# Sixteen weight conversions: one of four VectorE operations goes to GpSimd

## The chip, the cores and the metric

The kernel runs on one core of one Trainium2 chip. The metric is the device time of one execution in microseconds (us). The core has a matrix engine (TensorE, PE in the profile, with its weight loads as PEld), VectorE (DVE), ScalarE (ACT), GpSimd (POOL) and SyncE (SP), which issues the DMAs. Each engine works through its own list of instructions in order, and waits at the head of the list until the data and the buffer of the next instruction are free. SBUF is the on-chip working memory. PSUM is the memory into which TensorE writes; GpSimd has no operand there in this kernel.

## The reference

Attention over 32 memory slots, for 8 batches of 8 heads, 576 positions and 64 dimensions, and then two feed-forward layers on 4608 tokens:

```
a   = softmax over the positions of phi            # [b, h, 576, 32]
k_m, v_m = a^T k, a^T v                            # [b, h, 32, 64]
p   = softmax over the 32 slots of q k_m^T / 8
x   = p v_m                                        # 4608 x 512
h = x @ w1;  x = (h - tanh(h)) @ w2                # 512 -> 2048 -> 512
h = x @ w3;  out = where(h > 0, h, exp(min(h, 0)) - 1) @ w4
```

The weights arrive as 64-bit floats. The kernel builds 32-bit floats from their two 32-bit words.

## The kernel before, in words

**Weights.** `convert` (line 41) makes a 128x512 tile of 32-bit floats of a tile `raw` of 64-bit words. The high word is clamped and shifted to give the sign, the exponent and the upper bits of the mantissa, and the low word gives the rest. ScalarE takes the absolute value of the high word into a PSUM tile `cv_m` (line 48), VectorE clamps it (line 50), shifts and masks it (line 51), puts the sign in (line 54) and the low bits (line 57). In a "whole" conversion (the first eight tiles of `w1`) that is the weight. In the others the result stands in an SBUF tile `cv_a`, ScalarE rounds it to the high half of the weight (line 62), and GpSimd subtracts that to get the low half (line 64). `cv_m` has one buffer, `cv_a` two, `raw` three. There are 64 conversions; the first 16 are those of `w1` and `w2` for the first half of the hidden columns (four pairs of tiles of each).

**Attention.** 16 units, each one batch and four heads (line 118), with the tiles named in the profile: `cmax`, `mT`, `dmax`, `bmax` for the maximum over positions, `a`, `km`, `kk`, `vbd` for the memories, `pq`, `qT`, `sc`, `s`, `smax`, `pT`, `phl` for the scores and their softmax. A unit ends with the DMA of `phl` to `p` (units 0 and 1, line 246) and to DRAM, from where later blocks load `p` (line 329).

**Layer 1.** 64 blocks of 288 tokens with a quarter of the hidden columns each. A block has two halves. In each: `h_ps` on TensorE (line 375), `t`, `u`, `s`, `big` on ScalarE (lines 386 to 397), `v` on GpSimd (393), three operations on VectorE (402 to 404), `g` on ScalarE and GpSimd (410, 411), and `x_ps` on TensorE (423), which runs four products behind. `vw` (line 360) is the product of memories and `w1`, which `h_ps` needs. **Layer 2** follows from block 60 on.

**The order of the work.** The program is written out in one thread. Units and conversions are Python generators: each `yield` ends a stage, and `Staged.round()` takes every live generator one stage on. The loop over blocks calls `cv.round()` and `cv.half()` for conversions and `units.round()` twice in every half. Unit starts stand in a table of round numbers (`units.at`). Where a block needs weights that are not converted yet, `need` calls `cv.round()` until they are, and in block 1 each such call takes the units on by a round too. So the number of stages of a conversion decides how its instructions and those of the units stand among those of the blocks.

Of the kernel before, what the change touches and what calls it, by code (L numbers as in the profile page):

```python
# [8 lines left out]
F32 = mybir.dt.float32  # L9
F32R = mybir.dt.float32r  # L10
I32 = mybir.dt.int32
U32 = mybir.dt.uint32
ACTF = mybir.ActivationFunctionType
ALU = mybir.AluOpType
# [21 lines left out]
def r32(ap):  # L36
    return ap.bitcast(F32)


def convert(nc, pool, psum, raw, dst, whole=False):  # L40

    words = raw.bitcast(U32)
    w_lo, w_hi = words[:, 0::2], words[:, 1::2]
    lo_lim = 2.0 ** -15
    hi_lim = float.fromhex("0x1.fffffep+16")
    m = psum.tile(list(w_hi.shape), F32, tag="c", name="cv_m")
    mu = m.bitcast(U32)
    nc.scalar.activation(m, w_hi.bitcast(F32), ACTF.Abs)
    yield
    nc.vector.tensor_scalar(m, m, hi_lim, lo_lim, op0=ALU.min, op1=ALU.max)  # L50
    nc.vector.tensor_scalar(mu, mu, 3, 0x3FFFFFFF, op0=ALU.logical_shift_left, op1=ALU.bitwise_and)
    yield
    a = pool.tile(list(w_hi.shape), F32, tag="a", name="cv_a")
    nc.vector.scalar_tensor_tensor(mu, w_hi, 0xC0000000, mu, op0=ALU.bitwise_and, op1=ALU.bitwise_or)
    if whole:
        a = dst()
    nc.vector.scalar_tensor_tensor(a.bitcast(U32), w_lo, 29, mu, op0=ALU.logical_shift_right, op1=ALU.bitwise_or)
    if whole:
        return
    yield  # L60
    hi, lo = dst()
    nc.scalar.activation(hi, a, ACTF.Copy)
    yield
    nc.gpsimd.tensor_tensor(lo, a, r32(hi), op=ALU.subtract)  # L64
# [484 lines left out]
def moe_kernel(tc, q, k, v, phi, w1, w2, w3, w4, out):  # L549
    nc = tc.nc  # L550
    with ExitStack() as top, tc.manual_schedule():
# [15 lines left out]
        cv_p = new(l1b, "cv", 2, side="right")  # L567
# [3 lines left out]
        cv_ps = new(top, "ps_c", 1, space=PSUM)  # L571
# [20 lines left out]
        def conv(layer, kind, pg, c, lead=2):  # L592

            w = {("i", 1): w1, ("o", 1): w2, ("i", 2): w3, ("o", 2): w4}[kind, layer]
            raw = raw_p.tile([128, 512], mybir.dt.int64, tag="raw", name="raw")
            if kind == "i":
                src = w.rearrange("(k p) f -> p k f", p=128)[:, 2 * c:2 * c + 2, 256 * pg:256 * pg + 256]
                nc.sync.dma_start(out=raw.rearrange("p (a f) -> p a f", a=2), in_=src)
            else:
                r0 = 256 * pg + 128 * c  # L600
                nc.sync.dma_start(out=raw, in_=w[r0:r0 + 128, :])
            for k in range(lead + 1):
                yield k == lead
            staged, whole = [], (layer, kind) == (1, "i") and pg < 4

            def dst():
                if layer == 1:
                    ws = wi if kind == "i" else wo
                    if c == 0:
                        pg2, odd = divmod(pg, 2)  # L610
                        if kind == "i":
                            ws[pg] = [wt_p[pg2 % 2].tile([128, 4, 256], F32 if whole else F32R, tag=f"wi{odd}a", name="w1")]
                            if not whole:
                                ws[pg].append(wt_p[2].tile([128, 4, 256], F32R, tag=f"wl{pg}", name="w1"))
                        else:
                            pool, tags = (wt_p[odd], "wi0b wi1b") if pg2 == 2 else (wt_p[pg2], f"wo{odd}a wo{odd}b")
                            ws[pg] = [pool.tile([128, 2, 512], F32R, tag=t, name="w1") for t in tags.split()]
                    if whole:
                        return part(ws[pg][0], c)
                    return [part(t, c) for t in ws[pg]]  # L620
                staged.append(wst_p[0].tile([128, 2, 512], F32R, tag="wst", name="wst"))
                return staged[-1][:, 0], staged[-1][:, 1]

            yield from convert(nc, cv_p, cv_ps, raw, dst, whole)
            converted.add((layer, kind, pg, c))
            if layer == 2:
                yield
                nc.sync.dma_start(out=w_dram[kind][pg, :, :, 512 * c:512 * c + 512], in_=r32(staged[-1]))

        conv_pair = lambda layer, kind, pg: [conv(layer, kind, pg, c) for c in range(2)]  # L630
        conv_l1 = lambda kind, *pgs: [g for pg in pgs for g in conv_pair(1, kind, pg)]
        conv_l2 = [g for pg in range(NPG) for kind in "io" for g in conv_pair(2, kind, pg)]
# [8 lines left out]
        for what in "phi", "kv", "q0", "q1":  # L641
            at0.load(0, what)
            at1.load(1, what)
        cv_first = [conv(1, "i", k // 2, k % 2, 0) for k in range(3)]
        cv = Staged([conv(1, "i", 1, 1)] + conv_l1("o", 0, 1), 2)
        cv.wait = 5
        for k, g in enumerate(cv_first):
# [140 lines left out]
        for bi, (ss, bp, sub, j) in enumerate(blocks):  # L788
# [50 lines left out]
            for i in range(2):  # L839
                pg = 2 * sw + i  # L840
# [107 lines left out]
```

## Time and profile before

| | before |
|---|---|
| median of three runs | 1695.24 us (1695.19 to 1697.84) |
| profiled execution, its own time | 1694.74 us |
| its span, first to last instruction | 1693.0 us |
| TensorE busy | 1616.4 us, 95% |
| VectorE, ScalarE, GpSimd busy | 1190.3, 930.6, 760.0 us |
| mean granted TensorE clock | 0.988 of full speed |

Busy shares are means over stages that differ: in the first 165 us the attention, the conversions and the first blocks share all engines, and TensorE is busy least there. A row of idle time names what ended it.

### The profile page before, as it was taken

The page shows a single profiled execution, that of the slowest core. Times are in us where ns is not written, and L with a number is a line of the kernel's source. Part 1 is how long each engine was busy: PE and PEld are TensorE (multiplying, and loading weights), DVE is VectorE, ACT ScalarE, POOL GpSimd, SP SyncE. Part 2 cuts the span into 40 slices and gives each one's busy share as a digit, 9 for nine tenths or more (in the row PEclk, how much of TensorE's full clock was granted, in tenths as well). Part 3 has the DMA queues.
Part 4 walks back from the last instruction along what each step waited for, and adds up shares of the span by engine and source line. Part 5 has one row for each costly group of instructions (what it writes and reads, how often), then busy time and mean ns, then how long its engine had stood idle before and what let it go on. Part 6 is the DMA issues. An engine that isn't in the chain of part 4 may idle for free.

```text
span 1693.0 us, 26754 instructions
## 1 busy us (share of the span) xinstructions
PE 1616.4 (95%) x9986; PEld 1400.3 (83%) x9986; DVE 1190.3 (70%) x1730; ACT 930.6 (55%) x1677; POOL 760.0 (45%) x540
## 2 busy tenths in 40 slices
PE   6778999899998999999999999999999999999998
PEld 4556888787898999999999888888888888888886
DVE  4887778677989999999865655655555556555554
ACT  2466777677788898988853333333333333333332
POOL 1245666566666776767652322222323223223222
PEclk9889999999999999999999999999999999999999
DMA  8875667576565566665588321212121212121100
GB/s 204 216 201 167 202 192 220 175 212 211 192 207 168 170 215 220 218 219 205 188 274 309 100 74 38 75 50 63 50 73 40 75 40 72 51 75 50 31 7 25
DMA packets 140922, 236.10 MB, mean 139 GB/s; under 512 B 8184, under 2 KB 102392, under 8 KB 138744
## 3 DMA queue, kind: packets, MB, share of 16 engines
q1 hardware_dynamic: 140792, 234.39, 43.6%
q8 instruction: 79, 1.29, 0.3%
q14 instruction: 51, 0.42, 0.1%
HBM read 158.73 MB, written 74.45 MB: 138 GB/s over the span
## 4 chain that ended last, share of the span: by engine, by line
PE 75%; DVE 8%; ACT 5%; DMA 4%; issue 4%; POOL 3%; SPq 0%; ACTq 0%; POOLq 0%; DVEq 0%
PE h_ps L484 24%; PE o_ps L526 23%; PE x_ps L423 16%; PE h_ps L375 8%; DMA raw<-in_moe_w_in_dram 2%; DVE s L403 1%; PE vw_ps L344 1%; PE vw_ps L360 1%; DMA phi<-in_phi_dram 1%; ACT t L386 1%; DVE h_ps L402 1%; DMA kv<-in_v_dram 1%; POOL v L393 1%; PE km L170 1%; DVE s L404 1%
## 5 line engine op out<-in xcount | busy, mean ns | idle before, releaser
L423 PE MATMUL x_ps<-g,w 128*128 128x288 f32 x3072 | 441.6, 297 | 12.9 <-POOL w L64 4.7
L510 POOL TENSOR_TENSOR e<-hm,e 128x512 fp32r<-128x512 f32 x144 | 187.0, 1299 | 577.0 <-ACT e L509 533.7
L423 PEld LDWEIGHTS x_ps<-g,w 128*128 128x128 f32 x3072 | 417.1, 189 | 26.9 <-ACT x L430 7.5
L484 PE MATMUL h_ps<-x,wi 128*128 128x512 f32 (+1 forms) x1920 | 424.6, 371 | 0.0
L526 PE MATMUL o_ps<-wo,e 128*128 128x512 f32 x1728 | 422.8, 393 | 0.7 <-POOL e L510 0.7
L484 PEld LDWEIGHTS h_ps<-x,wi 128*128 128x128 f32 x1920 | 336.1, 188 | 68.0
L526 PEld LDWEIGHTS o_ps<-wo,e 128*128 128x128 f32 x1728 | 323.3, 188 | 75.4 <-POOL e L510 1.1
L495 ACT ACTIVATE t_ps<-hm 128x512 f32<-128x512 f32 x144 | 86.7, 602 | 504.8 <-DVE hm L494 504.8
L393 POOL TENSOR_TENSOR v<-t,u 128x576 f32<-128x576 f32 x128 | 183.1, 1430 | 155.7 <-ACT u L387 141.3
L501 DVE SCALAR_TENSOR_TENSOR hm<-hm,t_ps 128x512 f32<-128x512 f32 x144 | 99.0, 688 | 201.2 <-ACT hm L496 201.2
L375 PE MATMUL h_ps<-p,vw 128*128 128x288 f32 x1536 | 234.9, 303 | 5.0 <-DVE s L404 3.0
L411 POOL TENSOR_TENSOR g<-s,g 128x576 fp32r<-128x576 f32 x128 | 201.2, 1572 | 82.9 <-ACT g L410 74.3
L375 PEld LDWEIGHTS h_ps<-p,vw 128*128 128x128 f32 x1536 | 214.3, 192 | 16.1 <-issue 10.4
L494 DVE TENSOR_SCALAR hm<-h_ps 128x512 f32<-128x512 f32 x144 | 99.6, 692 | 129.3 <-PE h_ps L484 128.6
L403 DVE SCALAR_TENSOR_TENSOR s<-s,v 128x576 f32<-128x576 f32 x128 | 141.8, 1108 | 7.3 <-POOL v L393 7.2
L386 ACT ACTIVATE t<-h_ps 128x576 f32<-128x576 f32 x128 | 83.3, 651 | 84.0 <-PE h_ps L375 36.6
L404 DVE COPY_PREDICATED s<-big,h_ps 128x576 f32<-128x576 uint32 x128 | 106.5, 832 | 12.1 <-DVE s L403 0.5
L388 ACT ACTIVATE s<-u,bias 128x576 f32<-128x576 f32 x128 | 99.6, 778 | 25.4 <-POOL g L411 15.8
L503 DVE TENSOR_TENSOR hm<-hm,h_ps 128x512 f32<-128x512 f32 x144 | 98.9, 687 | 5.0
L502 DVE SCALAR_TENSOR_TENSOR hm<-hm,t_ps 128x512 f32<-128x512 f32 x144 | 98.9, 687 | 5.0
L402 DVE TENSOR_TENSOR h_ps<-h_ps,t 128x576 f32<-128x576 f32 x128 | 96.7, 755 | 3.2 <-ACT u L387 3.2
L496 ACT ACTIVATE hm<-hm 128x512 f32<-128x512 f32 x144 | 91.1, 632 | 14.0 <-ACT t_ps L495 1.1
(96 smaller groups left out, 1703.7 us busy)
## 6 DMA issues: line engine op xcount, KB each, us to landing
x_dram<-x SPq DMA_DIRECT2D x128, 288.0 KB
xr<-x_dram SPq DMA_DIRECT2D x72, 512.0 KB
p<-p_dram SPq DMA_DIRECT2D x62, 576.0 KB
raw<-in_moe_w_in_dram SPq DMA_DIRECT2D x32, 512.0 KB
raw<-in_moe_w_out_dram SPq DMA_DIRECT2D x32, 512.0 KB
w_dram<-wst SPq DMA_DIRECT2D x32, 512.0 KB
kv<-in_k_dram SPq DMA_DIRECT2D x16, 576.0 KB
kv<-in_v_dram SPq DMA_DIRECT2D x16, 576.0 KB
```

Source lines behind the costliest of these rows:

```text
L375: nc.tensor.matmul(ps[:, j, :NB], lhsT=vw[a][:, kc, 128 * j:128 * j + 128], rhs=p[:, kc, b, :], start=(k == 0), stop=(k == 5))
L386: nc.scalar.activation(t, w[0], ACTF.Tanh)
L388: nc.scalar.activation(s, u, ACTF.Square, bias=bias[:, 0:1], scale=G_S)
L393: nc.gpsimd.tensor_tensor(v, t, u, op=ALU.mult)
L402: nc.vector.tensor_tensor(d, d, t, op=ALU.subtract)
L403: nc.vector.scalar_tensor_tensor(s, s, G_B, v, op0=ALU.add, op1=ALU.mult)
L404: nc.vector.copy_predicated(s, big.bitcast(U32), d)
L411: nc.gpsimd.tensor_tensor(g[:, 1], s, r32(g[:, 0]), op=ALU.subtract)
L423: nc.tensor.matmul(ps, lhsT=wo[pg][a][:, j, 128 * dm:128 * dm + 128], rhs=g[:, b, j, :], start=(k == 0), stop=(k == 11))
L484: nc.tensor.matmul(out, lhsT=w3[:, a, kc, 128 * j:128 * j + 128], rhs=x[:, b, kc, :], start=(i == 0), stop=(i == 11))
L510: nc.gpsimd.tensor_tensor(e[:, 1], hm, r32(e[:, 0]), op=ALU.subtract)
L526: nc.tensor.matmul(acc, lhsT=e[:, a, jj, 128 * tg:128 * tg + 128], rhs=w4[:, b, j, :], start=(k == 0 and jj == 0 and i == 0), stop=(k == l ...
```

## The change

For the first 16 conversions (`layer == 1 and pg < 4`) ScalarE writes the absolute value to `cv_a` in SBUF, GpSimd clamps it there in place, and after one `yield` VectorE shifts it from `cv_a` into `cv_m` and goes on with the two other operations. The clamp and one `yield` are gone from VectorE's part: a conversion has one stage fewer. The other 48 are as before.

```diff
-def convert(nc, pool, psum, raw, dst, whole=False):
+def convert(nc, pool, psum, raw, dst, whole=False, apart=False):
...
-    m = psum.tile(list(w_hi.shape), F32, tag="c", name="cv_m")
-    mu = m.bitcast(U32)
-    nc.scalar.activation(m, w_hi.bitcast(F32), ACTF.Abs)
-    yield
-    nc.vector.tensor_scalar(m, m, hi_lim, lo_lim, op0=ALU.min, op1=ALU.max)
-    nc.vector.tensor_scalar(mu, mu, 3, 0x3FFFFFFF, op0=ALU.logical_shift_left, op1=ALU.bitwise_and)
-    yield
-    a = pool.tile(list(w_hi.shape), F32, tag="a", name="cv_a")
+    if apart:
+        a = pool.tile(list(w_hi.shape), F32, tag="a", name="cv_a")
+        nc.scalar.activation(a, w_hi.bitcast(F32), ACTF.Abs)
+        nc.gpsimd.tensor_scalar(a, a, hi_lim, lo_lim, op0=ALU.min, op1=ALU.max)
+        yield
+        m = psum.tile(list(w_hi.shape), F32, tag="c", name="cv_m")
+        mu = m.bitcast(U32)
+        nc.vector.tensor_scalar(mu, a.bitcast(U32), 3, 0x3FFFFFFF, op0=ALU.logical_shift_left, op1=ALU.bitwise_and)
+    else:
...
-            yield from convert(nc, cv_p, cv_ps, raw, dst, whole)
+            yield from convert(nc, cv_p, cv_ps, raw, dst, whole, layer == 1 and pg < 4)
```

Lines behind `convert` have numbers that are 9 higher in the changed kernel. On VectorE, from the maximum `cmax` of unit 2 on, the first two conversions stand before like this (`s<-sc`, `nmax` and `dmax` belong to units):

```order
L129 TENSOR_REDUCE cmax<-phi 96x128
L50 TENSOR_SCALAR cv_m<-cv_m 128x512
L51 TENSOR_SCALAR cv_m<-cv_m 128x512
L220 STREAM_TRANSPOSE s<-sc 128x288
L142 TENSOR_REDUCE nmax<-mT 128x1
L54 SCALAR_TENSOR_TENSOR cv_m<-raw,cv_m 128x512
L57 SCALAR_TENSOR_TENSOR w_351<-raw,cv_m 128x512
L220 STREAM_TRANSPOSE s<-sc 128x288
L146 TENSOR_SCALAR dmax<-ident,nmax 128x128
L50 TENSOR_SCALAR cv_m<-cv_m 128x512
L51 TENSOR_SCALAR cv_m<-cv_m 128x512
```

and in the changed kernel, at the same place of VectorE, so:

```order
L138 TENSOR_REDUCE cmax<-phi 96x128
L53 TENSOR_SCALAR cv_m<-cv_a 128x512
L63 SCALAR_TENSOR_TENSOR cv_m<-raw,cv_m 128x512
L66 SCALAR_TENSOR_TENSOR w_334<-raw,cv_m 128x512
L229 STREAM_TRANSPOSE s<-sc 128x288
L151 TENSOR_REDUCE nmax<-mT 128x1
L229 STREAM_TRANSPOSE s<-sc 128x288
L155 TENSOR_SCALAR dmax<-ident,nmax 128x128
L53 TENSOR_SCALAR cv_m<-cv_a 128x512
```

Four operations in two groups have become three in one. On GpSimd, around the last two conversions of the 16 (`w_1380` is the low half of the last weight), the list before is:

```order
L155 TENSOR_TENSOR a<-phi,bm 96x4x6x32
L411 TENSOR_TENSOR g<-s,g 128x576
L231 TENSOR_TENSOR s<-s,smax 128x576
L393 TENSOR_TENSOR v<-t,u 128x576
L64 TENSOR_TENSOR w_1380<-cv_a,w_1379 128x512
L411 TENSOR_TENSOR g<-s,g 128x576
L64 TENSOR_TENSOR w_1380<-cv_a,w_1379 128x512
```

and the list of the changed kernel at this place of GpSimd (there the weight is `w_1364`, and line 49 is the last clamp):

```order
L420 TENSOR_TENSOR g<-s,g 128x576
L49 TENSOR_SCALAR cv_a<-cv_a 128x512
L164 TENSOR_TENSOR a<-phi,bm 96x4x6x32
L402 TENSOR_TENSOR v<-t,u 128x576
L73 TENSOR_TENSOR w_1364<-cv_a,w_1363 128x512
L240 TENSOR_TENSOR s<-s,smax 128x576
L420 TENSOR_TENSOR g<-s,g 128x576
L73 TENSOR_TENSOR w_1364<-cv_a,w_1363 128x512
```

The unit's `a` and `s` have each moved behind the block's operation that they preceded, and the clamp is new. On TensorE, at the first `vw` of block 1 (`sc`, `pq`, `km` and `mT` are units' products), before:

```order
L218 MATMUL sc<-qT,kT 64x288 x2
L195 MATMUL pq<-ident,q 128x96 x3
L170 MATMUL km<-kv,a 32x192 x24
L140 MATMUL mT<-ident,cmax 128x96
L360 MATMUL vw_ps<-w_826,vm 64x256 x4
```

and after, on TensorE at the same `vw` (here of `w_812`), five rows from the same `sc` on:

```order
L227 MATMUL sc<-qT,kT 64x288 x2
L369 MATMUL vw_ps<-w_812,vm 64x256 x4
L432 MATMUL x_ps<-g,w_528 128x288
L432 MATMUL x_ps<-g,w_529 128x288
L432 MATMUL x_ps<-g,w_528 128x288 x2
```

`need` is through one round sooner in block 1, so from there on every stage of a unit stands one unit round later among the blocks' instructions, until the last unit is done in block 24 (block 2 begins after 31 unit rounds, where it was 32).

## Rows read from the trace of the kernel before

**Rows 1.** Part 1 of the page: busy us, share, instructions.
```profile
PE 1616.4 (95%) x9986; PEld 1400.3 (83%) x9986; DVE 1190.3 (70%) x1730; ACT 930.6 (55%) x1677; POOL 760.0 (45%) x540
```
**Rows 2.** Stretches: length; busy us (instructions) by engine; PE clock, DMA share, GB/s.
```profile
29.00:64.00 35.00, 24.73 (x162) 16.80 (x163) 32.44 (x57) 10.76 (x24) 4.98 (x3) 0.90 0.62 172
64.00:96.00 32.00, 24.86 (x203) 18.65 (x202) 23.46 (x40) 17.44 (x33) 13.74 (x10) 0.79 0.79 208
96.00:131.00 35.00, 27.97 (x216) 21.91 (x217) 30.56 (x54) 21.80 (x43) 16.04 (x12) 0.95 0.81 217
131.00:165.00 34.00, 26.35 (x205) 21.21 (x205) 22.68 (x37) 19.19 (x40) 18.62 (x13) 0.90 0.52 153
165.00:500.00 335.00, 317.19 (x2606) 277.92 (x2606) 263.23 (x392) 251.09 (x490) 212.40 (x150) 0.99 0.64 200
```
**Rows 3.** Waits of ScalarE, first 165 us: total us, times, longest.
```profile
ACT cv_m L48 <- DVE w L57: 18.0, 5, 6.1
ACT cv_m L48 <- DVE cv_a L57: 13.4, 3, 6.3
```
**Rows 4.** The clamp, line 50, by stretch: length, VectorE busy us (count).
```profile
29.00:64.00 35.00, 4.16 (x6) 0.90 0.62 172
64.00:96.00 32.00, 2.80 (x4) 0.79 0.79 208
96.00:131.00 35.00, 2.80 (x4) 0.95 0.81 217
```
**Rows 5.** Timeline of VectorE: start us, us, line, operation [idle before <-releaser].
```profile
54.12 0.69 DVE L50 TENSOR_SCALAR cv_m<-cv_m 128x512 f32<-128x512 f32 x1
54.85 0.70 DVE L51 TENSOR_SCALAR cv_m<-cv_m 128x512 uint32<-128x512 uint32 x1
55.46 0.75 DVE L239 TENSOR_TENSOR phl<-pT,phl 128x576 fp32r<-128x576 f32 x1
56.12 0.77 DVE L234 STREAM_TRANSPOSE pT<-s 128x576 f32<-128x576 f32 x1
...
59.51 0.76 DVE L239 TENSOR_TENSOR phl<-pT,phl 128x576 fp32r<-128x576 f32 x1 [1.30 <-ACT phl L238]
```
**Rows 6.** Timeline of ScalarE, columns as in rows 5.
```profile
58.81 0.67 ACT L238 ACTIVATE phl<-pT 128x576 fp32r<-128x576 f32 x1
...
86.85 0.61 ACT L62 ACTIVATE w<-cv_a 128x512 fp32r<-128x512 f32 x1
```
**Rows 7.** Timeline of TensorE, columns as in rows 5.
```profile
87.81 4.21 PE L70 MATMUL sc<-ident 128*128 128x128 f32 x18 [2.98 <-ACT qT L197]
...
147.87 0.67 PE L423 MATMUL x_ps<-g,w 128*128 128x288 f32 x3 [2.28 <-POOL w L64]
150.99 0.85 PE L423 MATMUL x_ps<-g,w 128*128 128x288 f32 x2 [2.44 <-POOL w L64]
...
375.60 2.64 PE L170 MATMUL km<-kv,a 96*32 96x192 f32 x48 [2.29 <-ACT a L161]
```
**Rows 8.** Timeline of GpSimd, columns as in rows 5.
```profile
136.76 1.87 POOL L155 TENSOR_TENSOR a<-phi,bm 96x768 f32<-96x768 f32 x1 [0.56 <-ACT bm L153]
138.59 1.44 POOL L411 TENSOR_TENSOR g<-s,g 128x576 fp32r<-128x576 f32 x1
144.06 1.16 POOL L231 TENSOR_TENSOR s<-s,smax 128x576 f32<-128x576 f32 x1 [4.04 <-ACT big L397]
...
149.66 1.27 POOL L64 TENSOR_TENSOR w<-cv_a,w 128x512 fp32r<-128x512 f32 x1
```
**Rows 9.** Groups of GpSimd by line, whole span: count | busy us, mean ns | idle before.
```profile
L64 POOL TENSOR_TENSOR w<-cv_a,w 128x512 fp32r<-128x512 f32 x24 | 32.0, 1334 | 1.1 <-ACT w L62 1.1
...
L146 POOL TENSOR_SCALAR dmax<-ident,nmax 128x128 f32<-128x128 f32 x10 | 7.6, 756 | 0.0
...
L98 POOL MEMSET kT<- 128x256 f32 x2 | 0.6, 309 | 0.0
```
**Rows 10.** Groups of VectorE by line, first 170 us, columns as in rows 9.
```profile
L403 DVE SCALAR_TENSOR_TENSOR s<-s,v 128x576 f32<-128x576 f32 x10 | 9.9, 986 | 1.3 <-POOL v L393 1.3
...
L402 DVE TENSOR_TENSOR h_ps<-h_ps,t 128x576 f32<-128x576 f32 x10 | 7.5, 754 | 0.0
...
L224 DVE TENSOR_TENSOR s<-s,smax 128x576 f32<-128x576 f32 x6 | 5.5, 925 | 0.2
```

More of the change, by code (lines that the diff above doesn't have):

```diff
@@ L45, in convert @@
     hi_lim = float.fromhex("0x1.fffffep+16")
-    m = psum.tile(list(w_hi.shape), F32, tag="c", name="cv_m")
-    mu = m.bitcast(U32)
-    nc.scalar.activation(m, w_hi.bitcast(F32), ACTF.Abs)
-    yield
-    nc.vector.tensor_scalar(m, m, hi_lim, lo_lim, op0=ALU.min, op1=ALU.max)
-    nc.vector.tensor_scalar(mu, mu, 3, 0x3FFFFFFF, op0=ALU.logical_shift_left, op1=ALU.bitwise_and)
-    yield
-    a = pool.tile(list(w_hi.shape), F32, tag="a", name="cv_a")
+    if apart:
[7 more added lines that the diff above has]
+    else:
+        m = psum.tile(list(w_hi.shape), F32, tag="c", name="cv_m")
+        mu = m.bitcast(U32)
+        nc.scalar.activation(m, w_hi.bitcast(F32), ACTF.Abs)
+        yield
+        nc.vector.tensor_scalar(m, m, hi_lim, lo_lim, op0=ALU.min, op1=ALU.max)
+        nc.vector.tensor_scalar(mu, mu, 3, 0x3FFFFFFF, op0=ALU.logical_shift_left, op1=ALU.bitwise_and)
+        yield
+        a = pool.tile(list(w_hi.shape), F32, tag="a", name="cv_a")
     nc.vector.scalar_tensor_tensor(mu, w_hi, 0xC0000000, mu, op0=ALU.bitwise_and, op1=ALU.bitwise_or)
```

## The prediction

> **What bounds the kernel now.** I read part 1 of the page first: TensorE is busy 95% of the span, so whatever shortens another engine's work counts only where TensorE stands idle for it [rows 1]. The table by stretches says where that is. From 165 to 500 us TensorE is busy 317.2 of 335 us; from 29 to 165 us it is busy 24.7 of 35, 24.9 of 32, 28.0 of 35 and 26.4 of 34, so 32 of 136 us are idle there, and all 16 changed conversions run in it [rows 2, 4]. In the same rows VectorE is busy 32.4 of 35 us from 29 to 64 and 30.6 of 35 from 96 to 131: there it sets the pace. From 64 to 96 no engine does alone, and from 131 to 165 VectorE is down to 22.7 of 34. The waits of ScalarE then show the one buffer of `cv_m`: eight times the absolute value of the next conversion stood at the head of ScalarE's list until VectorE had finished the one before, 18.0 and 13.4 us in all [rows 3]. Everything queued behind it on ScalarE (`qT`, the exponentials, `phl`) waited too. What is saved before 165 us stays saved as long as TensorE's work behind it is the same and its idle time there (17.8 of 335 us) does not grow.
>
> **The change part by part.** The sum is made against the profiled execution, 1694.74 us (span 1693.0 and 1.74 around it), which is 0.5 us under the median of the runs shown.
>
> *Units 0 and 1, 29 to 64 us.* Six clamps go [rows 4], five of them ahead of the last `phl` of unit 1, whose DMA the first `h_ps` waits for. From the start of one to the start of the next VectorE operation a clamp takes 0.73 us [rows 5]. The first four stand in a nearly gapless list: 4 x 0.73 = 2.9 us. The tail I work out anew. From the fifth clamp at 54.12 to the `phl` at 59.51 are 5.39 us [rows 5], with two operations of the conversion, `phl`, `pT`, the two other operations, and 1.30 us of waiting for ScalarE's `phl`, which had stood behind an absolute value in its list. After the change: three operations of 0.72 (2.16), `phl` 0.66 and `pT` 0.70 (by their starts), ScalarE's `phl` 0.67 [rows 6] and 0.2 for the handing over make 4.39. That is 1.0 us less. Term: -3.9.
>
> *64 to 96 us.* Four clamps go here, but TensorE, VectorE and ScalarE hand over to each other, and only some of it counts. I take one clamp, 0.73. The high half `w` of a conversion (0.61 us at 86.85) stood in ScalarE's list before the `qT` for which TensorE then waited 2.98 us [rows 6, 7]; a stage earlier it no longer does: 0.6. Term: -1.3 (bounds 0 and the four clamps and two such steps, -4.1).
>
> *96 to 131 us.* Four clamps, 4 x 0.73 = 2.9 us, on an engine that is busy 87% of the stretch [rows 2, 4]: -2.6.
>
> *131 to 165 us.* TensorE's `x_ps` waits twice, 2.28 and 2.44 us, for the low halves of the last two conversions from GpSimd [rows 7]. GpSimd's list from `s` at 144.06 ends with the second of them at 150.93 [rows 8]; the five operations stay, in another order, and start with `v`, which does not need VectorE's sums of `s`. What stands ahead is `g`, the last clamp and `a`. `g` can start when its input from ScalarE is there, about 137.2; with 1.44 for `g`, about 2 until the clamp is done (its absolute value ended at about 139.4, and 1.3 for itself), and 1.87 for `a`, `v` starts at about 142.6. So the list is through 1.5 us sooner. Term: -1.5 (bounds +1.0, if the clamp takes 2.5 us more than I think, and -4.7, both waits).
>
> *The clamp on GpSimd.* No row shows a GpSimd operation with two constants on 128x512. The nearest is the subtraction of the same shape, 1.33 us with two inputs [rows 9]. Below, a memset of 128x256 takes 0.31, so 0.6 for 512 columns; above, four times the 128x128 `dmax`, 0.76 each, 3.0. I take 1.3. Ahead of unit 2 GpSimd has nothing to do (5.0 of 35 us busy from 29 to 64 [rows 2]), so the first six cost nothing there and only have to be done one stage later, when VectorE wants them. The ten others have 52.6 us of idle time from 64 to 165 around them. A clamp queues `v`, `g` and `a` behind itself; their cover is that idle time. VectorE's shift waits for the clamp in place of ScalarE; what would wait behind it is the block's next operation on VectorE.
>
> The Trainium skill, "GPSIMD Engine Reference", section 3.1, gives 769 ns as measured for the best case of its elementwise loop over 512 elements. No run here shows it yet; by it the clamp would be at 0.8, and the sum 0.5 us lower through the next term.
>
> *VectorE and GpSimd at the same time.* VectorE's line 403, which reads two SBUF tiles, takes 0.99 us where line 402 of the same size, with one operand in PSUM, takes 0.75 [rows 10]; line 224 reads two as well, 0.93. GpSimd is busy 48.4 of 101 us from 64 to 165 [rows 2], and that costs such an operation 0.23 us. The clamps add 16 x 1.3 = 20.8 us of GpSimd to 136 us, a share of 0.15: 0.23 x 0.15 / 0.48 = 0.07 us for each of 16 operations (lines 403 and 224). Term: +1.2 (bounds 0 and +3, at 3.0 a clamp).
>
> The Trainium skill, "SBUF — State Buffer", section "Who interferes with whom", says that a VectorE instruction with two SBUF inputs contends with a GpSimd instruction that reads SBUF, and that the one that issues second blocks until the other ends. The 0.99 against 0.75 agrees that it costs something. Were each of the 16 clamps to meet one such operation for its whole length, the cost would be 16 x 1.3 = 21 us in place of 1.2; the rows do not bear that out, since `v` and `g` with 48% of GpSimd's time cost 0.23 a piece.
>
> *The shift by one unit round.* From block 2 to block 24 the units' stages stand one unit round later. Units start in odd and in even rounds already, so both positions occur before; I cost it at 0, with 3 us to either side: 17.8 us of TensorE's idle time are there to be had or added to [rows 2]. DMAs: units' loads and the stores of `phl` move with them; the load of `p` for a block is issued one or two blocks ahead still. The moved absolute value frees `raw` sooner, so weights are loaded sooner. ScalarE's operation writes SBUF where it wrote PSUM, and VectorE's shift reads SBUF; rows 5 and 6 show 0.6 to 0.7 us for this size from either, so 0.
>
> Sum: -3.9 - 1.3 - 2.6 - 1.5 + 1.2 = -8.1, so 1686.6, rounded 1687 us.
>
> **The rivals.**
>
> *A. Only the first stretch pays.* Behind 64 us the blocks are a ring through four engines, and a shorter VectorE just waits for the others. For it: TensorE's waits there end with ScalarE and GpSimd [rows 7]. Against: VectorE is busy 87% from 96 to 131. Then -3.9 + 1.2 = -2.7: 1692.0. The same class holds a slow clamp, 3.0 us: ten of them behind 64 us with 1.7 more each are 17 us on GpSimd, of which, at a GpSimd that is idle for half of the time, a third or so comes onto the way: +6, 1692.6. For that: `dmax` with a quarter of the columns already takes 0.76 [rows 9].
>
> *B. Slower: the units fall badly.* One round later a unit's `a` reaches ScalarE and GpSimd behind the block's work, and TensorE stands at `km`, which is in its list ahead of the block's products. Its price is in the trace once: 2.29 us at 375.60 [rows 7]. Twelve units run behind block 2. Were half of them to meet it, 6 x 2.3 = 13.8 us: 1686.6 + 13.8 = 1700.4. From five units on (1698.1) nothing is gained. Against it: before, units of either parity run through the same places and met it once.
>
> *C. More than I count.* TensorE's granted clock is at 0.79 of full speed from 64 to 96 and 0.90 from 131 to 165 [rows 2], following its idle time; if the shorter waits keep it up and both waits for the low halves go, 5 us more: 1682.
>
> **How the numbers follow.** This kernel's runs tell 0.2%, 3.4 us, from no change: faster is under 1691.9, slower over 1698.6. Forecast with C: 0.60. A: 0.24, at the lower edge of no change, of which 0.03 I give to faster. B: 0.16, with 0.01 in no change. So faster 0.63, same 0.22, slower 0.15. The range goes from 1680 (C and a lucky shift) to 1699; 0.07 is left out below, 0.13 above. The forecast's own range is 1681 to 1691.
>
> **What would show it.** Right: the first `h_ps` starts about 4 us sooner, near 59.9; the waits of ScalarE's absolute value for VectorE are gone; VectorE's busy time is down by about 10 us; the clamp takes 1.0 to 1.6 us; `x_ps` waits for the low halves 3 us or less in all; the stretch from there to the end is as long as before within 3 us. Wrong: VectorE waits at line 53 for GpSimd by more than 5 us in all, the clamp takes 2 us or more, or TensorE's idle time from block 2 to block 24 grows by more than 5 us.

## The result and the profile after

The changed kernel is slower: 1713.55 us (median of 4 runs, 1709.95 to 1719.05) against 1695.22 us before (four runs), a ratio of 1.0111 with a 95% interval of 1.009 to 1.0132. The prediction was 1687.0, faster. The profiled execution took 1709.95 us with a span of 1708.1, 15.1 more than before. The tables below are of the changed kernel; lines behind `convert` are 9 higher in it.

Part 1 of its page, answering to [rows 1]: VectorE has lost 8.6 us of work, GpSimd has gained 10.5, TensorE is as busy as before in a longer span.

```profile
PE 1616.6 (95%) x9986; PEld 1401.3 (82%) x9986; DVE 1181.7 (69%) x1714; ACT 930.9 (54%) x1677; POOL 770.5 (45%) x556
```

The stretches of [rows 2], columns as there:

```profile
29.00:64.00 35.00, 26.81 (x187) 19.02 (x186) 27.59 (x50) 12.95 (x27) 7.82 (x9) 0.90 0.71 204
64.00:96.00 32.00, 21.03 (x201) 16.15 (x199) 24.59 (x40) 16.89 (x33) 17.59 (x15) 0.95 0.78 198
96.00:131.00 35.00, 27.55 (x216) 22.16 (x217) 28.95 (x50) 23.17 (x46) 21.14 (x18) 0.95 0.71 203
131.00:165.00 34.00, 28.30 (x220) 24.83 (x217) 24.72 (x36) 20.19 (x42) 20.30 (x15) 0.90 0.55 161
...
165.00:500.00 335.00, 301.54 (x2446) 261.12 (x2445) 242.29 (x366) 233.02 (x458) 198.48 (x140) 0.96 0.61 190
```

Up to 165 us the kernel is ahead. Matching the 128 operations `t<-h_ps` of ScalarE one by one, in one execution of each kernel, the changed kernel leads by 3.3 us at the first, 4.3 at block 2, 5.5 in the second half of block 4 and 2.5 to 3.3 in block 8. It is the last row that turned: TensorE is busy 301.5 us there, where it was 317.2. Two places make the loss. Between the halves of block 9 a lead of 5.6 us becomes a lag of 5.4, and between the halves of block 19 a lead of 0.7 becomes a lag of 13.3. These are 11.0 and 14.0 us, 25 together; 6.1 of the first came back in between, and after the second the lag is 12.3 to 16.7 to the end. TensorE's timeline, changed kernel (start, us, operation, idle before and who ended it), with the first `h_ps` ahead and the two places last:

```profile
60.49 1.70 PE L384 MATMUL h_ps<-p,vw 128*128 128x288 f32 x11 [2.73 <-DMA p<-phl]
...
88.85 1.08 PE L369 MATMUL vw_ps<-w,vm 128*64 128x256 f32 x6 [3.53 <-DVE w L66]
...
145.48 0.85 PE L432 MATMUL x_ps<-g,w 128*128 128x288 f32 x2 [4.00 <-POOL w L73]
...
236.59 0.39 PE L149 MATMUL mT<-ident,cmax 96*128 96x96 f32 x1 [7.51 <-DVE cmax L138]
...
395.53 1.23 PE L227 MATMUL sc<-qT,kT 128*64 128x288 f32 x4 [8.11 <-DVE vw L372]
```

Behind both stands VectorE, whose list is in order and whose head was `cmax`, waiting for a unit's input `phi` from DRAM. At 393.43 it is the same `cmax` that holds up the `vw` behind it. VectorE, changed kernel:

```profile
235.00 1.44 DVE L138 TENSOR_REDUCE cmax<-phi 96x128 f32<-96x768 f32 x1 [7.62 <-DMA phi<-in_phi_dram]
...
393.43 1.44 DVE L138 TENSOR_REDUCE cmax<-phi 96x128 f32<-96x768 f32 x1 [7.71 <-DMA phi<-in_phi_dram]
```

The chain of waits through the first of these (start, us, what) shows how long the transfer took, changed kernel:

```profile
219.42 1.86 POOL a L164
221.30 13.68 DMA phi<-in_phi_dram
235.00 1.45 DVE cmax L138
```

and the chain of the kernel before at the same unit (10):

```profile
222.12 2.49 DMA phi<-in_phi_dram
```

The trace has an event for each share of a DMA that has arrived, and the last of them is its landing. By these events that transfer took 3.0 us before and 13.7 now; that of unit 15 took 3.1 and 13.5. Unit 10's was issued 0.8 us sooner than before, unit 15's, behind the first loss, 9.6 us later; both stand at another place in SyncE's list. SyncE's DMA issues (start, us of issuing), kernel before:

```profile
222.12 0.32 SPq L112 DMA_DIRECT2D phi<-in_phi_dram  x1
222.49 0.53 SPq L329 DMA_DIRECT2D p<-p_dram  x1
```

and changed kernel:

```profile
215.63 0.53 SPq L338 DMA_DIRECT2D p<-p_dram  x1
217.17 0.74 SPq L447 DMA_DIRECT2D x_dram<-x  x1
221.30 0.32 SPq L121 DMA_DIRECT2D phi<-in_phi_dram  x1
...
227.54 1.97 SPq L338 DMA_DIRECT2D p<-p_dram  x1
```

Before, `phi` went just ahead of a block's load of `p`; now, one round later, it follows one by 5.7 us (4.8 us at unit 15). And a load of `p` is slow: its landing comes 12.4 us after its issue (median of 23 between 165 and 500 us, 9.1 to 19.4; 12.2 before), and 17.8 and 15.2 us after it for the two ahead of these `phi`. The trace's packets say why. Between 225.2 and 226.0 us only packets of 4608 bytes move, which are rows of `p`, beside one of instructions, and the DMA share is 0.29 of 16 engines, about four and a half (stretch of the changed kernel, columns as in rows 2):

```profile
225.20:226.00 0.80, 0.80 (x8) 0.80 (x7) 0.70 (x2) 0.77 (x2) 0.00 (x0) 1.00 0.29 108
```

Of the 384 packets of that `phi` 288 went at 222 to 224 us and the last 96, a quarter, at 231 to 235. Its landing events agree: twelve of the 16 came by 224.84, the other four from 232.65 to 234.98. So four of the 16 DMA engines had `p`, and what was queued behind it, to move first; the other twelve had long done their share of `phi`. A whole load of `p` has five landing events, one soon after its issue and four at its end, where every other DMA from 165 to 500 us has 16. The source of a `p` load is four groups of 32 rows (line 338).

### The profile page after: what moved, and what is told of

It is laid out like the page before. It is cut to its first block, busy times and chain, and to the rows that moved or that the text cites. A ratio compares the mean times of both kernels' runs of the same rounds, so it can differ in the third digit from the quotient of the medians.

```text
span 1708.1 us, 26769 instructions
## 1 busy us (share of the span) xinstructions
PE 1616.6 (95%) x9986; PEld 1401.3 (82%) x9986; DVE 1181.7 (69%) x1714; ACT 930.9 (54%) x1677; POOL 770.5 (45%) x556
## 4 chain that ended last, share of the span: by engine, by line
PE 71%; DVE 7%; POOL 6%; DMA 6%; issue 5%; ACT 4%; SPq 0%; POOLq 0%; DVEq 0%; ACTq 0%
PE h_ps L493 23%; PE o_ps L535 23%; PE x_ps L432 13%; PE h_ps L384 7%; DMA phi<-in_phi_dram 2%; POOL g L420 2%; POOL v L402 1%; DVE s L412 1%; PE vw_ps L369 1%; POOL a L164 1%; PE vw_ps L353 1%; PE km L179 1%; DVE h_ps L411 1%; DMA p<-p_dram 1%; DMA raw<-in_moe_w_in_dram 1%
## 5 line engine op out<-in xcount | busy, mean ns | idle before, releaser
L432 PE MATMUL x_ps<-g,w 128*128 128x288 f32 x3072 | 445.9, 299 | 13.3 <-POOL w L73 5.1
L384 PEld LDWEIGHTS h_ps<-p,vw 128*128 128x128 f32 x1536 | 213.7, 192 | 18.3 <-issue 12.2
L406 ACT ACTIVATE big<-u,bias 128x576 f32<-128x576 f32 x128 | 98.0, 765 | 2.0 <-DVE s L413 2.0
```

What stands on the lines that cost most here:

```text
L384: nc.tensor.matmul(ps[:, j, :NB], lhsT=vw[a][:, kc, 128 * j:128 * j + 128], rhs=p[:, kc, b, :], start=(k == 0), stop=(k == 5))
L432: nc.tensor.matmul(ps, lhsT=wo[pg][a][:, j, 128 * dm:128 * dm + 128], rhs=g[:, b, j, :], start=(k == 0), stop=(k == 11))
```

## The experiments

Each is compared with the kernel before on the same chip: 1695.11 us for the first four, 1694.37 for the next four, 1694.26 for the last. Ratios carry their 95% interval. The unit rounds, the clamps and the loads of `p` are varied apart. The times of `e1`, `e2`, `e3` and `e8` came out 0.2 to 1.2 us above the ranges expected for the theory that each bears out.

**The lost stage given back** (`e1`): the clamp stays on GpSimd, and the units stand where they stood.

```diff
         mu = m.bitcast(U32)
         nc.vector.tensor_scalar(mu, a.bitcast(U32), 3, 0x3FFFFFFF, op0=ALU.logical_shift_left, op1=ALU.bitwise_and)
+        yield
```

> The change with a second yield between the shift and the two other VectorE operations, so that the stages of conversions and units are counted as before the change (block 2 begins after 32 unit rounds), and the clamp is still on GpSimd. Theory T1 (the lost stage lets a load of p be issued ahead of the load of phi of units 10 and 15, and phi lands 10 us late): 1686 to 1693 us, phi of unit 10 lands within 5 us, and TensorE has no idle time of over 4 us behind 165 us. Rival T2 (the clamp on GpSimd costs it, by its time, its waits and its contention): 1705 us or more, as in the changed kernel.

Measured: 1693.75 us, ratio 0.9999 (0.9978 to 1.002). `phi` of units 10 and 15 lands in 3.0 and 3.1 us, and SyncE's list has its old order. The stretch from 165 to 500 us, `e1`:

```profile
165.00:500.00 335.00, 317.23 (x2605) 277.99 (x2606) 263.47 (x390) 250.92 (x491) 212.17 (x150) 0.99 0.65 202
```

TensorE's 317.2 us of [rows 2] are back, with all 16 clamps on GpSimd. The loss is not the clamp's.

**The stage alone taken away** (`e2`): the kernel before, clamps on VectorE, one stage fewer for the 16 conversions.

```diff
     nc.scalar.activation(m, w_hi.bitcast(F32), ACTF.Abs)
-    yield
+    if not apart:
+        yield
     nc.vector.tensor_scalar(m, m, hi_lim, lo_lim, op0=ALU.min, op1=ALU.max)
```

> The kernel before with one yield less in the first 16 conversions and all four operations left on VectorE (clamp, shift, sign and low bits in one go). T1: as slow as the changed kernel or slower, since the first 165 us gain nothing: 1708 to 1720 us, with two waits of VectorE's cmax for phi of 6 us or more. T2: as before the change, 1692 to 1698 us.

Measured: 1720.94 us, ratio 1.016 (1.0115 to 1.0205), no faster than the change itself (their intervals overlap). Both transfers are late again; the chain of waits, `e2`:

```profile
225.25 14.14 DMA phi<-in_phi_dram
...
384.04 13.48 DMA phi<-in_phi_dram
```

The lag jumps in blocks 9 and 19, by 12.0 and 14.0 us, as it does in the changed kernel. The shift of one round is enough to make the loss.

**The units caught up** (`e3`): the changed kernel, with one round of the units put back in block 1, and the conversions as short as in the change.

```diff
                     need("i", vpg, bi == 1)
+                    if (bi, i) == (1, 0):
+                        units.round()
```

> The changed kernel with one unit round more in block 1, so that the units stand among the blocks as before the change, while conversions keep the stage less and the clamp on GpSimd. T1: 1684 to 1692 us, phi of units 10 and 15 lands within 5 us. T2: 1705 us or more. A second rival T3 (the conversions, which come a stage sooner, are what collides, not the units): 1705 us or more here, and 1690 in the run with the stage put back.

Measured: 1693.15 us, ratio 0.9989 (0.9966 to 1.0011). `phi` lands in 3.2 and 3.0 us. With `e1` this brackets the clamp's own worth in this kernel: between a gain of 0.34% and a loss of 0.2%.

**`p` in four** (`e4`): the changed kernel, units late, but each load of `p` as four DMAs of 32 rows.

```diff
-        self.nc.sync.dma_start(out=r32(t).rearrange("p r t s -> p (r t s)"),
-                               in_=self.p_dram[n // 2, :, :, n % 2].rearrange("g q m f -> (g q) m f"))
+        flat = r32(t).rearrange("p r t s -> p (r t s)")
+        for g in range(2):
+            for q in range(2):
+                r0 = 64 * g + 32 * q
+                self.nc.sync.dma_start(out=flat[r0:r0 + 32], in_=self.p_dram[n // 2, g, q, n % 2])
```

> The changed kernel with each load of p from DRAM issued as four DMAs of 32 partitions in place of one of 128; the order of SyncE's list stays. If phi is late because a load of p keeps a few of the 16 DMA engines busy for 10 us (T1 with that mechanism): loads of p spread over all engines, phi of units 10 and 15 lands within 6 us of its issue, 1684 to 1695 us. If it is late only by the bytes that are queued ahead of it, whatever engines they use: 1707 us or more. Three issues more for each of 62 loads cost SyncE about 0.5 us each, some 90 us of its time, and nothing on the path.

Measured: 1689.44 us, ratio 0.9967 (0.9948 to 0.9985). The order in SyncE's list is the bad one still, `e4`:

```profile
216.26 2.91 SPq L342 DMA_DIRECT2D p<-p_dram  x4
219.26 0.38 SPq L450 DMA_DIRECT2D x_dram<-x  x1
222.24 0.33 SPq L121 DMA_DIRECT2D phi<-in_phi_dram  x1
```

but all four parts of a `p` have landed 6.9 us after the first issue (median), and `phi` lands in 2.9 and 3.4 us. The `mT` of unit 10, which waited 7.51 us, has no idle time ahead of it, `e4`:

```profile
229.95 0.30 PE L149 MATMUL mT<-ident,cmax 96*128 96x96 f32 x1
```

So it takes both: the new order, and a `p` that only a few DMA engines move.

**The same in the kernel before** (`e5`, the diff of `e4` applied to it).

> The kernel before, with each load of p written as four DMAs of 32 partitions. Theory (the loss is phi behind a load of p, and before has no such pair): hardly any change, 1693 to 1697, every phi lands in 3 to 6 us as it did, and the 1689.4 of the changed kernel with the same split is then the clamps' own gain of some 5 us. Rival (the split is worth something everywhere): 1688 to 1691, like the changed kernel with the split, and the clamps are worth nothing by the end of the program.

Measured: 1695.13 us, ratio 0.9998 (0.998 to 1.0016). The split by itself is worth nothing there. Beside `e4`'s 0.9967 this leaves some 0.3%, 5 us, for the moved clamps once `p` is out of the way. The two ran on different chips, and their intervals touch; `e8` below is the closer comparison.

**`phi` in a queue of its own** (`e6`): the changed kernel; ScalarE issues the loads of `phi` of unit 3 and later.

```diff
-            self.load(nxt, "phi")
+            self.load(nxt, "phi", nc.scalar)
             yield
         nc.scalar.activation(av, av, ACTF.Exp)
```

> The changed kernel, with the loads of phi of units 2 to 15 issued by ScalarE in place of SyncE, at the same place of the program, so in a queue of their own. Theory a (phi stands behind p in SyncE's queue, and packets of one queue go in order on each DMA engine): phi of units 10 and 15 lands in under 6 us, no jump at blocks 9 and 19, 1688 to 1695. Theory b (the few DMA engines that move p are themselves taken, whatever the queue): phi takes 8 to 14 us still, and the time stays at 1705 to 1714.

Measured: 1723.11 us, ratio 1.0152 (1.0115 to 1.0189), worse than either theory said. Thirteen loads moved, those of units 3 to 15; unit 2's, which the expectation counts too, stayed. In the ten that were issued while a `p` was under way `phi` took 5.4 to 12.5 us. Where no `p` was, it took 3.1 to 5.9. VectorE's waits from 165 to 500 us, `e6` (us in all, times, longest):

```profile
DVE cmax L138 <- DMA phi<-in_phi_dram: 22.7, 7, 7.3
```

In the changed kernel this row reads 15.3 us in 2, before it was 3.0 in 2 (both shown below). So the order within SyncE's queue is not all of it: `phi` of another queue is held up as well, and at more units, for its issue now follows ScalarE's list and meets other loads of `p`. That a queue of its own helps at equal issue times isn't excluded, since these moved too. The Trainium skill, "DMA: Bandwidth & Descriptors", section "Issuing engines are not separate DMA queues", says that transfers run on the same 16 engines and interleave there whoever starts them; these times agree.

**Only two loads of `p` in four** (`e7`): the changed kernel; the ninth and nineteenth load of `p`, those ahead of the two `phi`.

```diff
+        self.p_loads = getattr(self, "p_loads", 0) + 1
+        if self.p_loads in (9, 19):
```

> The changed kernel, with only two loads of p written as four DMAs each: the ninth and the nineteenth that SyncE issues, which stand ahead of phi of units 10 and 15. Theory (these two pairs are the whole loss): phi of units 10 and 15 lands in 3 to 5 us, both jumps go, and the time is 1688 to 1695, at most 4 us over the kernel with every p split (1689.4). Rival (p loads in general hold up other transfers too, and the two are only the most visible): one jump goes or both shrink, 1698 to 1708.

Measured: 1705.80 us, ratio 1.0064 (1.0046 to 1.0083): the rival's number. Both jumps shrink, from 11.0 and 14.0 us to 9.2 and 10.3. My theory was too narrow. SyncE's list, `e7`:

```profile
209.14 2.32 SPq L455 DMA_DIRECT2D x_dram<-x  x1
211.50 2.83 SPq L618 DMA_DIRECT2D raw<-in_moe_w_out_dram  x1
215.75 0.32 SPq L124 DMA_DIRECT2D q<-in_q_dram  x1
216.12 6.59 SPq L344 DMA_DIRECT2D p<-p_dram  x4
224.70 0.38 SPq L455 DMA_DIRECT2D x_dram<-x  x1
225.20 0.39 SPq L121 DMA_DIRECT2D phi<-in_phi_dram  x1
```

Two whole loads of `p`, issued at 196.85 and 197.96, had landed by 206.0 and 215.6, but the shares of the later DMAs that stood behind them on the same four engines had not: of the `raw` issued at 211.50 twelve arrived by 220.84 and the last at 228.0. Meanwhile the issuing itself is slow: the four parts take 6.59 us to issue, where they took 2.91 in `e4`, and `phi` is issued 3 us later and lands in 7.6. The load of `p` that delays a `phi` is not only the last one; what is queued for the few engines carries over for some 30 us, from the load at 197.96 to 228.0.

**Both repairs** (`e8`: `e3` and `e4` together).

> The changed kernel with one more round of the units in block 1 (so that every stage stands where it stood before) and every p split in four. If the split's 3.7 us over that round alone (1693.15 to 1689.44) come from transfers that wait behind p wherever the units stand: 1687 to 1690, no different from the split alone. If the split only repaired what the shifted round had broken, the units' places being repaired already here: 1692 to 1695.

Measured: 1690.20 us, ratio 0.9973 (0.9956 to 0.9989). It is as good as `e4`, and both beat the kernel before; the place of the units no longer matters once `p` is split. `e8` and `e5` ran ten times each on one chip, have the units at the same places and `p` in four, and differ in the moved clamps and the shorter conversions alone: 1690.20 us (1687.42 to 1692.56) against 1695.13 (1692.35 to 1698.23). So these are worth 4.9 us, 0.3%, where `p` is in four; with `p` whole, `e3` does not tell their worth from nothing. Where in the program they are gained is not shown: in the two traces `e8` and `e5` are level in block 4.

**`p` in four by columns** (`e9`): as many DMAs as in `e4`, but each takes all four groups of rows.

```diff
+        for c in range(0, 1152, 288):
+            self.nc.sync.dma_start(out=flat[:, c:c + 288], in_=src[:, :, c:c + 288])
```

> The changed kernel with each load of p as four DMAs again, but cut along the columns: each still takes all four groups of 32 rows, 288 of the 1152 columns. Theory a (a DMA is dealt out to the 16 DMA engines by its outermost dimension, which is 4 here, so that four engines carry each of the four again): phi of units 10 and 15 lands 8 us or more after its issue, p itself takes 15 us or more, and the time is 1703 to 1720. Theory b (what counts is that the load is in four pieces with smaller packets, so that others get between): phi lands in 3 to 5 us, p in under 10 us, and the time is 1686 to 1695, as with the split by rows.

Measured: 1708.77 us, ratio 1.0091 (1.0065 to 1.0116). A `p` is whole 10.8 us after its first issue (median; 15.4 and 14.6 for the two ahead of these `phi`), and `phi` is late again, landing in 9.3 and 8.1 us; chain of waits, `e9`:

```profile
226.73 9.30 DMA phi<-in_phi_dram
```

Theory a holds for the time and for `phi`; the 15 us or more that it gave `p` are met only about these two. Four DMAs whose outermost dimension is 4 behave like the one, four with 32 rows outermost do not. Each piece by columns has five landing events, as the whole load has, and each piece by rows 16. The Trainium skill, "DMA: Bandwidth & Descriptors", section "Why a DMA increments its semaphore by 16 and not by 1", states the rule: a transfer runs on the largest number of engines, up to 16, that divides the slowest dimension of both sides. That is 4 for the whole load and for the columns, and 16 for the rows; 1708.8 against 1689.4 us agrees.

## Why the prediction was wrong

**The step that failed** is the shift by one unit round: "both positions occur before; I cost it at 0", and within it "the load of `p` for a block is issued one or two blocks ahead still". The second is true and beside the point. What counted was not when `p` is needed, but which transfer stands behind it in SyncE's list. I bounded the step by 3 us; by `e2` the shift alone costs 1.6%, and the changed kernel is 20 us over `e3`, which lacks it. That both positions occur before was an argument for safety only if both had been looked at: in the kernel before, `phi` of units 9, 11, 12 and 14 was issued 6 to 11 us behind a load of `p` that was still on the way, and landed 6.0 to 9.4 us after its issue; ahead of units 8, 10, 13 and 15 the last load of `p` had landed, and they took 3.0 to 3.3. The price stood in the trace, but VectorE came to `cmax` late enough at those units to hide it. Its wait from 165 to 500 us (us in all, times, longest) was, before:

```profile
DVE cmax L129 <- DMA phi<-in_phi_dram: 3.0, 2, 1.6
```

and it is in the changed kernel:

```profile
DVE cmax L138 <- DMA phi<-in_phi_dram: 15.3, 2, 7.7
```

**Rival B** had the side and the cause in the large, the units' new places. Its mechanism was another: not `km` waiting for `a` at 2.29 us six times, but two inputs some 10 us late each. TensorE's `km` waited for `a` 3.3 us in 3 times from 165 to 500 us before, and 3.2 in 3 now. B's 13.8 us are short of the 25 that the two places cost.

**-3.9 for 29 to 64 us** measured -3.3 at the first `h_ps`: 60.49 in the timeline above, and in TensorE's of the kernel before

```profile
63.77 1.83 PE L375 MATMUL h_ps<-p,vw 128*128 128x288 f32 x12 [1.50 <-DMA p<-phl]
```

Right but for 0.6 in this pair of traces, and that is partly luck. `e3`, `e4`, `e7`, `e8` and `e9` have the changed kernel's instructions up to there and start the first `h_ps` at 60.98, 61.27, 61.19, 62.72 and 62.70 us; `e5`, there the kernel before, starts it at 62.41. By the means of six and two traces, 61.6 and 63.1, the term is 1.5 us, not 3.9. ScalarE's waits of [rows 3] for `cv_m` are gone from the first 165 us.

**-1.3 and -2.6 for 64 to 131 us** were too much: from the first `t` on the lead grows from 3.3 to 4.3 at block 2 and 3.8 at block 3, in place of another 3.9. VectorE now waits for ScalarE and for the clamp in a row, and I had put no price on that. Its waits in the first 165 us, changed kernel:

```profile
DVE cv_m L53 <- POOL cv_a L49: 13.1, 5, 6.8
```

and before the change, for ScalarE's absolute value:

```profile
DVE cv_m L50 <- ACT cv_m L48: 7.6, 6, 4.6
```

Most of the 13.1 us is that value still. The longest wait, 6.77 us, ends at 66.30. ScalarE in the changed kernel:

```profile
64.93 0.64 ACT L48 ACTIVATE cv_a<-raw 128x512 f32<-128x512 f32 x1
```

and GpSimd, which stood idle for it:

```profile
65.66 0.61 POOL L49 TENSOR_SCALAR cv_a<-cv_a 128x512 f32<-128x512 f32 x1 [0.62 <-ACT cv_a L48]
```

At the second longest GpSimd was not idle:

```profile
82.33 2.34 POOL L164 TENSOR_TENSOR a<-phi,bm 96x768 f32<-96x768 f32 x1
84.62 1.42 POOL L420 TENSOR_TENSOR g<-s,g 128x576 fp32r<-128x576 f32 x1
85.99 0.63 POOL L49 TENSOR_SCALAR cv_a<-cv_a 128x512 f32<-128x512 f32 x1
```

Here the clamp stands behind `a` and `g` without a gap. VectorE waits 3.67 us for it, 2.0 of them until ScalarE's value is there at 85.01 and 1.0 for `g`; TensorE's `vw` at 88.85, in the timeline above, waits 3.53 us for the weight. By the starts and ends of all five waits 9.0 us went to ScalarE's value, 1.4 to what stood ahead on GpSimd and 2.8 to the clamps themselves. So GpSimd's idle time, which I had named as the cover, did cover these waits but for 1.4 us. Over 5 us at line 53 is a sign that I had named for a wrong prediction, but it is not where the loss lies: in `e1`, with all 16 clamps on GpSimd, the loss is gone.

**-1.5 for 131 to 165 us**: GpSimd's list is through with the last low half 5.5 us sooner, at 145.43 for 150.93 [rows 8], but TensorE is there sooner too and waits 4.00 and 1.10 us, 5.1 in place of 4.7 [rows 7]. No gain. The lead of 5.5 us in block 4 is what is left of the 8.1 predicted: 3.3 at the first `t` and 2.2 from there on. These 2.2 are not the clamps'. `e2`, which leaves the clamps on VectorE, gains 2.0 over the same way, and `e4`, `e7` and `e9` 2.1 to 2.2; with the units in their old places `e3` loses 0.3 and `e1` 3.5. So they go with the units' late places, and for the three terms behind 64 us (-5.4) no gain is shown. Why `e1` loses so much there was not tested.

**The clamp at 1.3 us** was twice too long. All 16 of the changed kernel (minimum, median, maximum in ns):

```profile
L49 POOL TENSOR_SCALAR cv_a<-cv_a x16: 607/612/1127, 24.5 to 134.8; 128x512 f32<-128x512 f32 x16
```

0.61 us is my lower bound, from the memset of [rows 9]. The upper bound supposed a time that grows with the columns; `dmax`, with a quarter of them, has a median of 0.61 us itself (599 to 1113 ns). The Trainium skill's 769 ns ("GPSIMD Engine Reference", section 3.1) is over it too; the measurement decides. The rival of a slow clamp is out.

**+1.2 for VectorE and GpSimd at the same time** came near in size. Groups of VectorE in the first 170 us, changed kernel:

```profile
L412 DVE SCALAR_TENSOR_TENSOR s<-s,v 128x576 f32<-128x576 f32 x10 | 10.5, 1046 | 1.4 <-ACT x L439 0.7 <-POOL v L402 0.7
...
L411 DVE TENSOR_TENSOR h_ps<-h_ps,t 128x576 f32<-128x576 f32 x10 | 7.5, 752 | 3.9 <-ACT u L396 3.9
L233 DVE TENSOR_TENSOR s<-s,smax 128x576 f32<-128x576 f32 x6 | 5.8, 971 | 0.2
```

Against [rows 10] the two that read two SBUF tiles take 0.06 and 0.05 us more, 0.9 in all, and the one with an operand in PSUM none. But only two of these 16 run beside a clamp at all, for 1.1 us together, and the mean of line 412's ten is 0.94 us in `e1` and 1.00 in `e3`, which have the same clamps. So the 0.9 us is not told from scatter, and the term is not shown.

**Rival C**, a higher clock, came in part: from 64 to 96 us the granted clock is 0.95 for 0.79. It is lost again where TensorE stands idle for `phi`: idle from 229.1 us on, it is granted 0.50 from 234 to 235, the lower of its two levels, 1.2 GHz. Means of 25 us, changed kernel:

```profile
225.00:250.00 25.00, 17.05 (x149) 13.51 (x148) 13.12 (x22) 11.17 (x22) 7.77 (x7) 0.86 0.69 197
...
375.00:400.00 25.00, 15.76 (x137) 11.35 (x135) 14.82 (x24) 10.75 (x21) 11.19 (x8) 0.80 0.74 236
```

and the kernel before:

```profile
225.00:250.00 25.00, 23.21 (x205) 19.82 (x204) 18.75 (x30) 18.74 (x38) 14.47 (x12) 1.00 0.81 226
...
375.00:400.00 25.00, 22.54 (x183) 17.71 (x184) 14.70 (x28) 15.25 (x32) 10.31 (x9) 0.93 0.75 234
```

TensorE loses 6.2 and 6.8 us of work in these two stretches of 25 us, 12.9 of the 15.7 that it loses from 165 to 500.

## What to carry to other kernels

A change that takes a stage out of one stream moves every other stream that is counted in rounds; write down the DMA queue's list before and after, and for each transfer that is needed soon ask what it now follows and how many DMA engines that moves on. An operation that is put between two engines waits for the one and holds up the other, however idle its own engine is: look at when its input comes and at what stands ahead of it at that moment. Before a lead of a few us in one trace is explained, see how far traces of the same instructions lie apart. Where a position occurs more than once in the trace, take its price from the occurrences that something else hides.

## What was not expected of the hardware

A DMA of 576 KB whose outermost dimension is 4 lands after 12.4 us (median), and a 288 KB transfer behind one lands after 13.7 us in place of 3.0. Four DMAs of 32 rows land the same bytes in 6.9 us, and four of a quarter of the columns in 10.8. In `e7` a DMA that was issued 13.5 us after such a load still had its last four shares 3 to 7 us behind the other twelve. GpSimd's operation with two constants on 128x512 takes 0.61 us, less than half of its two-input operation of the same size (1.33 us [rows 9]).
